# Windowed attention and a SiLU expert on one core: PSUM banks of the expert layers chosen by a longer eviction time, and one load of batch 0 moved from SP's queue to POOL's

## The chip, the core and the metric

The kernel runs on one core of a Trainium2 chip. Five engines work side by side, each on its own list of instructions in a fixed order, and wait for one another through semaphores: TensorE (PE in the profile; its weight loads are PEld), VectorE (DVE), ScalarE (ACT), GpSimd (POOL) and SyncE (SP). POOL and SP issue the DMA transfers here: POOL's go to a software queue (q0 in the profile) and can change the type on the way, SP's to a hardware queue (q1). Matmul results land in PSUM, which has eight banks of 128 partitions by 512 fp32 values. The metric is the device time of one execution in microseconds (us).

## What is computed

Attention in a causal window of 64 positions, over 8 batches and 8 heads with 576 positions and head size 64, and then an expert of two layers on the 4608 rows that result:

```python
def _attn_ref(q, k, v):                        # each (8, 8, 576, 64)
    scores = np.matmul(q, k.transpose(0, 1, 3, 2)) / np.sqrt(64)
    rel = pos[:, None] - pos[None, :]
    scores = np.where((rel >= 0) & (rel < 64), scores, -1000000000.0)
    attn = np.exp(scores - np.max(scores, axis=-1, keepdims=True))
    attn = attn / (np.sum(attn, axis=-1, keepdims=True) + 1e-09)
    return np.matmul(attn, v)

def _moe_ref(x, w_in, w_out):                  # x (4608, 512), w_in (512, 2048), w_out (2048, 512)
    h = x @ w_in
    g = h * (1.0 / (1.0 + np.exp(-h)))
    return g @ w_out
```

Inputs and output are fp32; the kernel computes in bf16 with fp32 sums.

## The kernel before

**Planning.** The kernel is written as operations with dependencies, an assumed duration on each engine that may run them, and a rank by class. `Plan.run` plays these through at build time and so fixes the order of instructions on each engine. An operation's `seen` is the time at which the plan takes its result as visible: its end plus `lat` for engine work (0.08 unless said otherwise), and for a transfer a begin on a modelled pipe plus `dma`. An operation that writes PSUM names a pool of banks (`at`: 0 to 3, `pv`: 4 and 5, `mp`: 4 to 7, `all`: 0 to 7). The plan gives it an idle bank, one whose last reader is `seen`, and of these for pool `mp` first banks 6 and 7, then 4 and 5, each time the one that has been idle longest. In the trace banks 0 to 3 are called `at` and 4 to 7 `mp`. On the chip only the order and the banks are left of this: real waits go by semaphores.

**Batch 0.** q and k of batch 0 come in eight loads, two heads each: q0, k0, q1, k1, q2, q3, k2, k3, where the number is the pair of heads. The first three (q0, k0, q1) are issued by SP as fp32 (L232), and an engine casts them to bf16 (L235). The other five are issued by POOL with the cast in the transfer (L229). TensorE transposes two loads at a time against an identity (L282), and ScalarE and VectorE copy the transposes out of PSUM, half each (L289). Then follow six units of scores (L311 adds the mask as a bias, L319 the product of q and k), exp on ScalarE (L337), the product with v (L349), and on VectorE the reciprocal (L356), the scaling (L359) and a transpose into `bridge` (L363), the expert's input. Until the last exp of batch 0, TensorE fills gaps with matmuls on zeros (L595).

**Later batches.** q and k come by POOL in 32-partition pieces (L239) and are transposed by VectorE (L246). The scores (L331) use banks 0 to 3, the product with v (L349) banks 4 and 5.

**Loads.** All of POOL's transfers go through one queue with eight outstanding: a ninth issue waits for the landing of the one eight before. Their order is q and k of batch 0, v of batch 0 (L253), w_in (L259), then q, k and v of batch 1 mixed with eight pairs of w_out's row blocks (L265), then the later batches.

**The expert.** Nine tiles of 512 rows (tile 0 takes the first 576 rows in two parts for the first layer, tile 1 what is left). The first layer (L369) sums four matmuls into one bank for each of 16 column blocks, and ScalarE's Silu (L375) reads the bank. The second layer (L381) sums 16 matmuls into a bank for each of four row blocks (tile 0 has all four open at once), the result is copied out (L387) and stored by SP (L391). The matmuls of the expert are one list in a fixed order, lowest in rank. The attention of the next batch goes in between, mostly within the second layer: scores, then some 17 second-layer matmuls, then the product with v.

Of the kernel before, what the change touches and what calls it, by code (L numbers as in the profile page):

```python
# [8 lines left out]
FP32 = mybir.dt.float32  # L9
# [5 lines left out]
class Plan:  # L15
# [31 lines left out]
    def run(self):  # L47
        head = {c: 0 for c in self.queues}
        engines = sorted({e for q in self.queues.values() for op in q for e in op["us"]})
        free = {e: 0.0 for e in engines}  # L50
        can = {e: [c for c, q in self.queues.items() if any(e in op["us"] for op in q)] for e in engines}
        table, left = "exp", self.count
        pipe, sent = {True: 2.0, False: 0.0}, []
        events, order = [0.0], []
        while left:
            if not events:
                raise RuntimeError([(c, head[c], q[head[c]]["n"]) for c, q in self.queues.items() if head[c] < len(q)])
            now = self.now = heapq.heappop(events)
            while events and events[0] == now:
                heapq.heappop(events)  # L60
            moved = True
            while moved:
                moved = False
                for e in engines:
                    if free[e] > now:
                        continue
                    best, kept = None, set()
                    heads = [(self.queues[c][head[c]], c) for c in can[e] if head[c] < len(self.queues[c])]
                    for op, c in sorted(heads, key=lambda x: x[0]["first"]):
                        if e == "POOL" and op["dma"] and len(sent) >= 8 and sent[-8] > now:  # L70
                            continue
                        if e not in op["us"] or not self.done(op["deps"]) or (op["gate"] and not op["gate"]()):
                            continue
                        if op["pool"]:
                            idle = [i for i in self.pools[op["pool"]] if i not in kept and self.done(self.banks[i])]
                            if len(idle) < len(op["untils"]):
                                if op["pool"] != "mp":
                                    kept.update(self.pools[op["pool"]])
                                continue
                            idle.sort(key=lambda i: (op["pool"] == "mp" and i in self.pools["pv"],  # L80
                                                     max([u["seen"] for u in self.banks[i]], default=0.0)))
                            op["bank"] = idle[:len(op["untils"])]
                            for i, until in zip(op["bank"], op["untils"]):
                                self.banks[i] = until
                        best = (op, c)
                        break
                    if best is None:
                        continue
                    op, c = best
                    head[c] += 1  # L90
                    us = op["us"][e]
                    if op["table"] and op["table"] != table:
                        table, us = op["table"], us + 1.28
                    end = free[e] = now + us
                    soft = e == "POOL"
                    if op["dma"] is None:
                        op["seen"] = end + op["lat"]
                    elif soft:

                        begin = max(pipe[True], end + 1.4)  # L100
                        pipe[True] = begin + op["dma"] * (1.5 if pipe[False] > begin else 1.0)
                        op["seen"] = pipe[True] + op["lat"] + 1.2
                        sent.append(op["seen"])
                        heapq.heappush(events, op["seen"])
                    else:
                        begin = max(pipe[False], end + 1.0)
                        busy = pipe[True] > begin and c != "ld0"
                        pipe[False] = begin + op["dma"] * (1.6 if busy else 1.0)
                        if busy:
                            pipe[True] += 0.6 * op["dma"]  # L110
                        op["seen"] = pipe[False] + {"ld0": 0.5, "st": 1.2}.get(c, 3.0)
                    op["at"], op["cls"], op["by"] = now, c, e
                    order.append((op, e))
                    left -= c != "warm"
                    moved = True
                    heapq.heappush(events, end)
                    heapq.heappush(events, op["seen"])
        for op, e in order:
            op["fn"](e)
# [3 lines left out]
def kernel(ctx, tc, q, k, v, w_in, w_out, out):  # L123
    nc = tc.nc
# [103 lines left out]
    def load_first_cast(w, u, kk):  # L228
        nc.gpsimd.dma_start(out=natbs[w][:, 0:S], in_=two(u, kk))  # L229

    def load_first(i, u, kk):
        nc.sync.dma_start(out=nats[i][:, 0:2 * S].bitcast(FP32), in_=two(u, kk))  # L232

    def cast_first(e, i, w):
        copies[e](out=natbs[w][:, 0:S], in_=nats[i][:, 0:2 * S].bitcast(FP32))  # L235
# [178 lines left out]
    def add_first_batch():  # L414
        got = {}
        for what, u in FIRST_LOADS:
            if what == "v":
                add_v_loads(0, [u], [c_vv[0]])
                continue
            kk = "qk".index(what)  # L420
            w = n_nat[1] % NNB
            n_nat[1] += 1
            if (what, u) in FIRST_LOADS[0:3]:
                i = n_nat[0] % NN
                n_nat[0] += 1
                ld = p.add("ld0", {"SP": 0.45}, lambda _, i=i, u=u, kk=kk: load_first(i, u, kk), dma=0.69)
                ca = p.add("cast", {"ACT": 0.7, "DVE": 0.56}, lambda e, i=i, w=w: cast_first(e, i, w), [ld])
                nat_free[i] = [ca]
            else:
                ca = p.add("early" if (what, u) in FIRST_LOADS[3:7] else "dma0", {"POOL": 0.6}, lambda _, w=w, u=u, kk=kk: load_first_cast(w, u, kk), dma=0.74)  # L430
            got[what, u] = (w, ca)
            if (what, u ^ 1) not in got:
                continue
            a = u // 2
            ws, loaded = zip(*[got[what, 2 * a + i] for i in range(2)])
            tu = p.add("turn", {"PE": 0.6}, None, [*loaded, c_ident], lat=0.1, pool="all", nb=2)
            tu["fn"] = lambda _, tu=tu, ws=ws: turn_first(tu, ws)
            for i in range(2):
                tu["untils"][i].append(p.add("lift", {"ACT": 0.64, "DVE": 0.75}, lambda e, tu=tu, a=a, kk=kk, i=i:
                                             lift(e, tu, a, kk, i), [tu, c_k[0]]))  # L440
                kq_done[(0, a)] = kq_done.get((0, a), []) + tu["untils"][i]
# [89 lines left out]
    def add_tile(j):  # L531
# [18 lines left out]
        for i, (ft, lo, hi) in enumerate(work):  # L550
            have = [op for n in range((j * TT + hi + 191) // 192) for op in o_done[n]]
            g, si = gt[ft]
            bank = None
            for c in range(NDC):
                op = p.add("moe", {"PE": 0.0036 + (hi - lo) / 2400}, None,
                           have + win[ft] + (exps[0] if j == 0 else []), lat=0.1,
                           pool=None if c else "mp")
                bank = bank or op
                op["fn"] = lambda _, bank=bank, ft=ft, c=c, lo=lo, hi=hi: first_layer(bank, j, ft, c, lo, hi)
                moe.append((op, 1, 1 if c == 0 and (i == 0 or hi > work[i - 1][2]) else -1))  # L560
            si.append(p.add("silu", {"ACT": 0.18 + (hi - lo) * 0.00083}, lambda _, bank=bank, g=g, lo=lo, hi=hi:
                            silu(bank, g, lo, hi), [op] + free_gt.get(g, []), table="silu"))
            bank["untils"][0] = [si[-1]]
        order = [(m, f, 0, d_model) for m in range(4) for f in range(NFT)]
        if j == 0:
# [4 lines left out]
        for i, (m, f, lo, hi) in enumerate(order):  # L570
# [7 lines left out]
            if f == NFT - 1:  # L578
                ot = n_ot[0] % NOT
                n_ot[0] += 1  # L580
                cp = p.add("out", {"DVE": 0.18 + (hi - lo) / 1000, "ACT": 0.18 + (hi - lo) / 1160},
                           lambda e, bank=bank[(m, lo)], ot=ot, lo=lo, hi=hi: copy_out(e, bank, ot, lo, hi),
                           [op, free_ot.get(ot)])
                bank[(m, lo)]["untils"][0] = [cp]
                free_ot[ot] = p.add("st", {"SP": 0.45}, lambda _, ot=ot, m=m, lo=lo, hi=hi: store(ot, j, m, lo, hi), [cp],
                                    dma=0.75 * (hi - lo) / d_model)
# [65 lines left out]
```

## Time and profile before

| | |
|---|---|
| device time, three runs | 302.37, 300.89, 302.20 us (median 302.2) |
| the profiled execution | 302.37 us, span of its instructions 300.6 us |
| TensorE busy | 287.4 us (96%) |
| ScalarE, VectorE, POOL busy | 176.8, 139.4, 117.0 us |
| first layer L369 busy, matmuls | 128.6 us, 696 |
| second layer L381 busy, matmuls | 124.2 us, 576 shown |
| Silu L375 | 174, 523 ns each |
| SP's loads of q in batch 0 (2), issue to landing | 4.7 us in the median |
| POOL's loads of k in batch 0 (3), issue to landing | 6.6 us in the median |

A row of the profile names the line, the engine, the operation, what it writes and reads, and in brackets how long the engine stood idle before it and what ended that. The chain of work that ended last is followed back from the last instruction: each piece is what the next one waited for, so a resource that the chain runs through sets the end. An engine that is not on the chain can be idle without cost. Matmuls overlap in the pipeline: one of 512 columns is shown with 0.38 us, but the next starts 0.216 us after it, so the spacing of the starts, not the length, is the rate. Some matmul records are missing.

### The profile page before, as it was taken

To read this page: it belongs to the slowest core of one execution; us is meant where nothing else is said; L and a number is where in the kernel's file an instruction comes from. 1 tells how busy PE (TensorE), PEld (TensorE's weight loads), DVE (VectorE), ACT (ScalarE), POOL (GpSimd) and SP (SyncE) were. 2 spreads that over 40 slices of the span, in tenths; PEclk is the share of its full clock that TensorE was granted. 3 is DMA by queue.
4 is the path that set the end of the run, shared out by engine and by line. 5 is a ranking of instruction groups with operands and counts; after the bars stand their busy time and mean duration, and the time that the engine had idled before them with its cause. 6 is when DMAs were issued, how large, how long until landed. Compare 5 with 4: busy or idle time off the path is not lost.

```text
span 300.6 us, 8485 instructions
## 1 busy us (share of the span) xinstructions
PE 287.4 (96%) x3609; PEld 150.4 (50%) x3641; DVE 139.4 (46%) x340; ACT 176.8 (59%) x341; POOL 117.0 (39%) x174
## 2 busy tenths in 40 slices
PE   7899999899999999999999999999999999999995
PEld 3566744785444544445444544454444544444444
DVE  3593377978886379327931693066006600000000
ACT  3697854886456745675477437753876376126511
POOL 8866976959898979860500000000000000000000
PEclk9799999999999999999999999999999999999999
DMA  7999999999999999992760210011001100020012
GB/s 174 176 203 169 131 165 170 225 136 129 171 179 141 109 188 172 148 94 74 81 71 0 74 39 34 2 37 72 35 0 39 72 35 2 35 77 29 2 70 71
DMA packets 82982, 28.78 MB, mean 96 GB/s; under 512 B 72448, under 2 KB 78080, under 8 KB 82944
## 3 DMA queue, kind: packets, MB, share of 16 engines
q0 software_dynamic: 77040, 17.92, 64.3%
q1 hardware_dynamic: 5904, 10.32, 9.8%
q8 instruction: 28, 0.46, 0.6%
q14 instruction: 10, 0.08, 0.1%
HBM read 36.70 MB, written 9.44 MB: 153 GB/s over the span
## 4 chain that ended last, share of the span: by engine, by line
PE 82%; DMA 8%; POOL 6%; issue 3%; ACT 1%; POOLq 0%; ACTq 0%
PE mp L381 39%; PE mp L369 37%; DMA w_out_sb<-in_moe_w_out_dram 5%; PE at L331 3%; PE mp L349 3%; DMA w_in_sb<-in_moe_w_in_dram 2%; POOL vv L253 2%; POOL w_in_sb L259 1%; POOL nat L239 1%; POOL w_out_sb L265 1%; POOL natb L229 1%; ACT ot L387 0%; ACT g L375 0%; PE at L349 0%; POOL ident L188 0%
## 5 line engine op out<-in xcount | busy, mean ns | idle before, releaser
L369 PE MATMUL mp<-bridge,w_in_sb 128*128 128x512 bf16 (+5 forms) x696 | 128.6, 342 | 1.8 <-ACT g L375 1.2
L381 PE MATMUL mp<-w_out_sb,g 128*128 128x512 bf16 (+2 forms) x576 | 124.2, 368 | 4.1 <-issue 3.3
L375 ACT ACTIVATE g<-mp 128x512 bf16<-128x512 f32 (+5 forms) x174 | 89.5, 523 | 30.9 <-PE mp L369 29.6
L369 PEld LDWEIGHTS <-w_in_sb 128*128 128x128 bf16 x696 | 66.3, 97 | 62.2 <-issue 7.6
L381 PEld LDWEIGHTS <-g 128*128 128x128 bf16 x608 | 55.9, 98 | 61.5 <-issue 0.7
L387 ACT COPY ot<-mp 128x512 f32<-128x512 f32 (+2 forms) x36 | 20.2, 563 | 62.1 <-PE mp L381 42.8
L340 DVE TENSOR_TENSOR e<-e,mask 128x384 bf16<-128x384 bf16 x84 | 26.0, 348 | 50.2 <-ACT e L337 49.7
L337 ACT ACTIVATE e<-at 128x384 bf16<-128x384 f32 x89 | 36.9, 497 | 16.0 <-PE at L331 15.9
L239 POOL DMA_DIRECT2D nat<-in_k_dram x56 | 34.6, 632 | 11.7 <-DMA vv<-in_v_dram 4.7
L253 POOL DMA_DIRECT2D vv<-in_v_dram x32 | 31.9, 1012 | 13.0 <-PE mp L349 12.9
L239 POOL DMA_DIRECT2D nat<-in_q_dram x56 | 34.8, 640 | 5.2 <-DMA w_out_sb<-in_moe_w_out_dram 3.2
L363 DVE STREAM_TRANSPOSE bridge<-ox 128x384 bf16<-128x384 bf16 x48 | 24.9, 553 | 0.0
L246 DVE STREAM_TRANSPOSE kt<-nat 128x576 bf16<-128x576 bf16 x28 | 20.7, 782 | 7.4 <-DMA nat<-in_k_dram 7.4
L246 DVE STREAM_TRANSPOSE qt<-nat 128x576 bf16<-128x576 bf16 x28 | 20.9, 789 | 1.3 <-DMA nat<-in_q_dram 1.2
L359 DVE TENSOR_TENSOR ox<-mp,rc 128x384 bf16<-128x384 f32 x43 | 21.3, 536 | 0.1
L356 DVE RECIPROCAL rc<-mp 128x6 f32<-128x6 f32 x43 | 8.0, 191 | 18.9 <-PE mp L349 18.3
L349 PEld LDWEIGHTS <-e 128*32 128x32 bf16 x1152 | 10.8, 95 | 9.0 <-issue 5.0
L299 DVE COPY vv<-vv 64x576 bf16<-64x576 bf16 (+1 forms) x14 | 7.3, 524 | 11.7 <-DMA nat<-in_k_dram 9.2
L349 PE MATMUL mp<-vv,e 128*32 128x65 bf16 x1032 | 12.2, 194 | 0.0
L331 PE MATMUL at<-qt,kt 32*128 32x64 bf16 x1008 | 11.6, 190 | 0.0
L331 PEld LDWEIGHTS <-kt 32*128 32x128 bf16 x1008 | 9.3, 92 | 4.3 <-issue 3.8
L337 ACT ACT_TABLE_LOAD x7 | 9.0, 1283 | 0.1
(55 smaller groups left out, 87.9 us busy)
## 6 DMA issues: line engine op xcount, KB each, us to landing
out_dram<-ot SPq DMA_DIRECT2D x35, 256.0 KB, 2.0
vv<-in_v_dram POOLq DMA_DIRECT2D x32, 144.0 KB, 5.6
nat<-in_q_dram POOLq DMA_DIRECT2D x56, 72.0 KB, 4.6
nat<-in_k_dram POOLq DMA_DIRECT2D x56, 72.0 KB, 4.0
w_out_sb<-in_moe_w_out_dram POOLq DMA_DIRECT2D x8, 256.0 KB, 7.6
w_in_sb<-in_moe_w_in_dram POOLq DMA_DIRECT2D x6, 256.0 KB, 7.3
nat<-in_q_dram SPq DMA_DIRECT2D x2, 288.0 KB, 4.7
w_in_sb<-in_moe_w_in_dram POOLq DMA_DIRECT2D x4, 128.0 KB, 6.0
```

The source lines that it names most:

```text
L239: nc.gpsimd.dma_start(out=nats[i][32 * h:32 * h + 32].rearrange("p (m x) -> p m x", m=NB), in_=(q, k)[kk][b, 4 * a + h].rearrange("(m p r) ...
L246: nc.vector.transpose(out=to[:, (2 * a + part) * S:(2 * a + part + 1) * S].rearrange("x (m t r) -> x m r t", t=32, r=2), in_=nats[i].rearr ...
L253: queue[e].dma_start(out=vv[b % NV][:, 2 * g0 + 1:2 * g1 + 1:2, 0:D], in_=v[b].rearrange("h s d -> (h s) d").rearrange("(g p) d -> p g d", ...
L331: nc.tensor.matmul(at_six(op["bank"][h])[:, a, x], lhsT=kt[b % NK][r, at:at + 128], rhs=qt[b % NK][r, at:at + 64], start=(s == a == x == 0 ...
L337: nc.scalar.activation(out=es[n % NE], in_=at_six(bank), func=ACTF.Exp, scale=scale)
L340: nc.vector.tensor_mul(es[n % NE], es[n % NE], mask0 if g == 0 else mask)
L349: nc.tensor.matmul(at_pv(bank)[32 * h:32 * h + 32, x, t], lhsT=e_of(b, a, n, h)[:, x, 32 * t:32 * t + 32], rhs=vv[b % NV][:, (4 * a + h) * ...
L359: nc.vector.tensor_mul(oxs[n % NOX], at_pv(bank)[:, :, :, 0:D], rcs[n % NRC].unsqueeze(3).to_broadcast([128, 3, 2, D]))
L363: nc.vector.transpose(out=bridge[:, n0:n0 + 3, 2 * a:2 * a + 2].rearrange("x t s (u i) -> x t s u i", u=2), in_=oxs[n % NOX].rearrange("p ...
L369: nc.tensor.matmul(banks[bank["bank"][0]][:, 0:hi - lo], lhsT=w_in_sb[:, c, ft * 128:(ft + 1) * 128], rhs=bridge[:, (j * TT + lo) // 64:(j ...
L375: nc.scalar.activation(out=gts[gt][:, lo:hi], in_=banks[bank["bank"][0]][:, 0:hi - lo], func=ACTF.Silu)
L381: nc.tensor.matmul(banks[bank["bank"][0]][:, 0:hi - lo], lhsT=gts[gt][:, m * 128:(m + 1) * 128], rhs=w_out_sb[:, f, lo:hi], start=(f == 0) ...
```

## The change

The change has two parts that touch the plan. The banks: Silu and copy-out operations of tiles 2 to 8 are planned with `lat` 0.22 instead of 0.08, so that a bank counts as taken for longer after its eviction; and once the last product with v is placed, every operation with a pool may take any of the eight banks. The loads: only q0 and k0 of batch 0 stay on SP; q1 goes to POOL with the cast in the transfer, ahead of k1, q2 and q3; the modelled times of SP's two loads are other ones.

```diff
                         if op["pool"]:
-                            idle = [i for i in self.pools[op["pool"]] if i not in kept and self.done(self.banks[i])]
+                            idle = [i for i in self.pools[op["pool"] if head["pv"] < len(self.queues["pv"]) else "all"] if i not in kept and self.done(self.banks[i])]
...
-                        busy = pipe[True] > begin and c != "ld0"
+                        busy = pipe[True] > begin
...
-                        op["seen"] = pipe[False] + {"ld0": 0.5, "st": 1.2}.get(c, 3.0)
+                        op["seen"] = pipe[False] + {"ld0": 1.2, "st": 1.2}.get(c, 3.0)
...
-            if (what, u) in FIRST_LOADS[0:3]:
+            if u == 0:
                 i = n_nat[0] % NN
                 n_nat[0] += 1
-                ld = p.add("ld0", {"SP": 0.45}, lambda _, i=i, u=u, kk=kk: load_first(i, u, kk), dma=0.69)
+                ld = p.add("ld0", {"SP": 0.45}, lambda _, i=i, kk=kk: load_first(i, kk), dma=-0.15 if kk == 0 else 0.7)
...
-                ca = p.add("early" if (what, u) in FIRST_LOADS[3:7] else "dma0", {"POOL": 0.6}, lambda _, w=w, u=u, kk=kk: load_first_cast(w, u, kk), dma=0.74)
+                ca = p.add("early" if (what, u) in FIRST_LOADS[2:6] else "dma0", {"POOL": 0.6}, lambda _, w=w, u=u, kk=kk: load_first_cast(w, u, kk), dma=0.74)
...
             si.append(p.add("silu", {"ACT": 0.18 + (hi - lo) * 0.00083}, lambda _, bank=bank, g=g, lo=lo, hi=hi:
-                            silu(bank, g, lo, hi), [op] + free_gt.get(g, []), table="silu"))
+                            silu(bank, g, lo, hi), [op] + free_gt.get(g, []), lat=0.22 if j > 1 else 0.08, table="silu"))
...
                            lambda e, bank=bank[(m, lo)], ot=ot, lo=lo, hi=hi: copy_out(e, bank, ot, lo, hi),
-                           [op, free_ot.get(ot)])
+                           [op, free_ot.get(ot)], lat=0.22 if j > 1 else 0.08)
```

In the order of instructions this gives: POOL issues q1, k1, q2, q3, then makes the identity, then issues k2 and k3 (before: k1, q2, q3, k2, the identity, k3). TensorE transposes q0/q1, k0/k1 and q2/q3, runs the first unit of scores, transposes k2/k3, runs four more units of scores and then the first product with v (before: all four transposes, four units of scores, the first product). First layers of tiles 2 to 7 use banks 4 to 7 and never the same one within two groups (before: mostly 6, 7, 6, 7); the rest of tile 7 and tile 8 use all eight. The number of matmuls on zeros stays 21. Behind the first matmul of the first layer the order on TensorE, ScalarE, VectorE, POOL and SP is the same as before but for the numbers of banks and of the `nat` buffers.

More of the change, by code (lines that the diff above doesn't have):

```diff
@@ L229, in load_first_cast, with load_first @@
         nc.gpsimd.dma_start(out=natbs[w][:, 0:S], in_=two(u, kk))
-    def load_first(i, u, kk):
-        nc.sync.dma_start(out=nats[i][:, 0:2 * S].bitcast(FP32), in_=two(u, kk))
+    def load_first(i, kk):
+        nc.sync.dma_start(out=nats[i][:, 0:2 * S].bitcast(FP32), in_=two(0, kk))
     def cast_first(e, i, w):
```

## The prediction

> **What bounds the kernel now.** I read the busy row first, then the chain that ended last, then the places where the chain leaves TensorE.
>
> ```profile
> PE 287.4 (96%) x3609; PEld 150.4 (50%) x3641; DVE 139.4 (46%) x340; ACT 176.8 (59%) x341; POOL 117.0 (39%) x174
> ```
>
> TensorE (PE) is the bound. No other engine passes 59%, so an edit counts only by the TensorE idle or waiting time that it takes away or adds. The chain shows two kinds of place:
>
> ```profile
> 13.54 7.20 DMA w_in_sb<-in_moe_w_in_dram
> 20.73 0.28 issue
> 21.02 8.23 DMA w_out_sb<-in_moe_w_out_dram
> ...
> 36.72 7.63 DMA w_out_sb<-in_moe_w_out_dram
> 44.36 0.04 issue
> 44.40 1.02 PE mp L381 x4
> ...
> 116.50 14.00 PE mp L369 x64
> ...
> 268.90 14.08 PE mp L369 x64
> ```
>
> Columns are start, length, what. Until 44.4 us the chain runs through POOL's queue of loads and ends on the fifth pair of w_out rows (issued at 36.72, landed at 44.36). From there it is TensorE, tile after tile. A first layer of a full tile (L369, 64 matmuls of 512 columns) takes 14.00 or 14.08 us. ScalarE's rows of the last tile show why that is not its floor:
>
> ```profile
> 271.54 0.60 ACT L375 ACTIVATE g<-mp 128x512 bf16<-128x512 f32 x1 [0.27 <-PE mp L369]
> 272.47 0.60 ACT L375 ACTIVATE g<-mp 128x512 bf16<-128x512 f32 x1 [0.33 <-PE mp L369]
> 273.33 0.60 ACT L375 ACTIVATE g<-mp 128x512 bf16<-128x512 f32 x1 [0.27 <-PE mp L369]
> 274.24 0.60 ACT L375 ACTIVATE g<-mp 128x512 bf16<-128x512 f32 x1 [0.31 <-PE mp L369]
> ```
>
> The starts are 0.93, 0.86 and 0.91 apart: every second group of four matmuls comes about 0.045 late. The start:
>
> ```profile
> 1.24 0.68 POOL L229 DMA_DIRECT2D natb<-in_k_dram  x1 [0.79 <-POOLq L636]
> 1.65 0.42 SPq L232 DMA_DIRECT2D nat<-in_q_dram  x1
> 8.12 0.67 ACT L235 CAST natb<-nat 128x576 bf16<-128x576 f32 x1 [3.09 <-DMA nat<-in_q_dram]
> 8.85 1.05 PE L282 MATMUL at<-ident,natb 128*64 128x128 bf16 x17 [2.33 <-ACT natb L235]
> ```
>
> SP's third load (q of heads 2, 3), issued at 1.65, lands at 8.10 and is cast until 8.79; TensorE's first transposes wait 2.33 us for it.
>
> **Part 1: the banks of tiles 2 to 8.** In the order of instructions before, the first layers fall into using banks 6, 7, 6, 7. A bank is then wanted again two groups later, 2 x 0.863 = 1.726 us (four matmuls at the measured pitch of 0.216). Its real turn is longer. In the last tile the group from 270.48 has its Silu at 271.54, 1.06 later; the Silu takes 0.60; the next matmul into the bank starts 0.07 after the Silu's end, at 272.21. The sum, 1.73, leaves nothing, and a Silu itself delayed delays the next group. So steps of 0.257 to 0.262 stand where 0.216 should, between matmuls of adjoining groups. I count 4 in each of tiles 2 to 7 and 6 in tile 8: 30 x 0.044 = 1.3 us. The second group of a tile is late by another 0.017 in six tiles: 0.1. Check by sums: the first nine groups of tile 2, whose banks come round after three groups or more, run at 0.863 each without a late step; against that pitch tile 2 loses 0.17, tiles 3 to 7 0.19 each, tile 8 0.27: 1.4 in all. In the new order no group of tiles 2 to 8 reuses a bank within two; three groups are 2.59 us against a turn of 1.73. **Saved: 1.4 us**, all on the bound. The bounds are 0 (if the handoff, not the bank, makes the late steps) and 1.4, since below 0.863 a group cannot go. I take 1.4, because tile 2 shows both reuses side by side.
>
> What else this moves: first layers now end on banks 4 and 5, which the next attention products (L349) need. Between them stand the scores and some 17 second-layer matmuls, 3.7 us; the Silu is done 1.1 + 0.6 = 1.7 after its group began. Nothing waits. The eight banks after attention put tile 8 on banks 0 to 3 too; three suffice, so this adds nothing. The orders of TensorE, ScalarE and VectorE are otherwise the same from the first first-layer matmul on.
>
> **Part 2: the third load moves from SP to POOL.** SP loses one issue (0.42), and its next instruction is a store at 53 us: nothing. ScalarE loses a cast of 0.67 at 8.12. POOL gains an issue ahead of all others, 0.57 to 0.68: the identity (done 3.9) comes at 4.5, before TensorE's first transpose at 6; the window and with it the bias (5.0) come 0.6 later, wanted at 9; the v issues from 4.91 and w_in from 8.85 come 0.6 later, but land 5 to 6 us after issue from a backlog, so this hides as long as the backlog lasts. VectorE and ScalarE swap halves of two copies (0.72 against 0.75): nothing. The nat buffers are used from one number earlier; each still waits for the batch two before, as now.
>
> Attention starts sooner. q now has POOL's first place, whose load (k) landed at 6.79 even against SP's third; the later places landed at 8.26, 8.92, 9.64 and 10.43. By these places, at the latest, the first transposes begin at 6.8 instead of 8.85, the second pair 8.3, the third 9.7, the first scores 10.4 instead of 13.1, and after one transpose group (0.69) and four more score groups (0.71 each, one now ahead of the first product) the first product starts at 14.7 instead of 15.97. If q lands at 5.8, as I expect without SP's third beside it, 13.8. VectorE's chain to the last bridge (16.48 to 23.42) follows the first product, so the first layer reaches steady running **1.3 to 2.2 us sooner**.
>
> The clock agrees with that. From 9.0 to 12.4 the granted clock was 0.50, behind the 2.33 us wait; three transpose groups took about 0.98 each where one at full clock took 0.69. The Trainium skill ("TensorE: Matmul & The Clock Gate", Part 1) halves the clock only after an idle window of about 3.4 us; by that this wait would have cost no clock, so by the page 0.9 us less would come back. The row stands against it.
>
> **But what is gained there is not kept.** At 44.40 TensorE waits for w_out's fifth pair:
>
> ```profile
> PE mp L381 <- DMA w_out_sb<-in_moe_w_out_dram: 0.2, 1, 0.2
> 44.40 1.02 PE L381 MATMUL mp<-w_out_sb,g 128*128 128x512 bf16 x4 [0.23 <-DMA w_out_sb<-in_moe_w_out_dram]
> ```
>
> It would have been there at 44.17. If it comes at 42.0 to 42.9, it waits till the pair lands, and the gain shrinks to how much sooner that is. All loads go through POOL's one queue, eight outstanding, so I ask how the queue shifts:
>
> ```profile
> q0 software_dynamic: 459, 0.47, 77.0%
> q1 hardware_dynamic: 145, 0.29, 25.0%
> ```
>
> This is the move of 4 to 8 us. The software queue moved 0.47 MB beside SP's third load; alone, from 7 us on, it moves 0.177 MB per us, in those 4 us 0.71. It carries 0.147 MB more now (0.8 us) and gets back up to 0.24 MB (1.4 us): 0.6 us sooner. Ends: 0.75 later (one more place at the observed step of 0.66 to 0.79, and no relief), 1.4 sooner (relief and no price). I take **0.5 us sooner**, near the sum, a little off for the ramp.
>
> The Trainium skill ("DMA: Bandwidth & Descriptors", Specifications) speaks against this half: it calls SP's path the faster one, 0.6 us to the first byte against about 1 us on GpSimd's. By the page this move costs some 0.4 us (an estimate). The rows say otherwise: SP's third landed 6.5 us after its issue, POOL's first 5.5.
>
> **Sum.** Profiled execution 302.37 us (span 300.61 and 1.76 around it): 302.37 - 1.4 - 0.5 = 300.5. The median shown, 302.2, is 0.2 below, so **300.3**. The three runs before reach from 300.89 to 302.37, so single times scatter by more than half of what I forecast. A change under 0.5% (1.5 us) can't be told from none.
>
> **Rivals.**
> - *The bank's part alone* (20%): the w_out pair lands no sooner, or up to 0.75 later. For it: one more transfer stands ahead of it in the queue. Against it: SP's share of 4 to 8 us is freed. 300.8 to 301.6.
> - *The whole start is kept* (15%): the pair lands 1 to 2.2 sooner, since the queue ran nearly dry from 29 to 32 us (POOL idle 1.65 before 29.53, waiting for a slot), and such a spell may close. 302.2 - 1.4 - 1.0 to 2.2: 298.6 to 299.8.
> - *Late steps stay* (6%): the 0.045 is the handoff's and not the bank's; the change doesn't do what it says. Against it: tile 2. 301.7.
> - *Slower* (4%): POOL's queue runs dry twice more behind the added transfer, as at 27.88 to 29.53. Price 2 x 1.65 + 0.75 = 4.1 at the w_out pair; it outweighs the banks from a landing at 45.8 and is measurably slower from 47.3. 302.2 - 1.4 + 4.1 = 304.9. Only one such spell is in the trace, so I think it unlikely.
>
> The forecast's own case (1.4 and 0.2 to 1.0) has 55%: 299.8 to 300.6. The range takes in the first two rivals and the third, with 0.3 for scatter at the top: 298.9 to 301.9. Faster by over 0.5% means below 300.7: most of the forecast's case (44), all of the whole start (15), a little of the first rival (3): 62%. Within 0.5%: 34%. Slower: 4%.
>
> **What would show it.** First layers of 13.8 us in the chain for tiles 3 to 8, Silu starts 0.86 apart. The first transposes at about 6 and no clock of 0.5 after 9. Steady first layer by 21 to 22. A wait of 1 to 2 us for w_out where 0.23 stood, its landing at 43.9. I am wrong if the 0.26 steps remain, if that pair lands after 45, or if a new wait stands between 44 and 60.

## The result

| | before | changed |
|---|---|---|
| median (range, runs) | 302.14 us (300.13 to 303.33, 6) | 298.65 us (297.99 to 299.08, 6) |
| profiled execution, its span | 302.37, 300.6 us | 298.62, 296.9 us |

The ratio is 0.9895, with a 95% interval of 0.9859 to 0.9932: 3.2 us faster (2.1 to 4.3). The direction was forecast, the size was not: 1.9 us were expected, and the median lies 0.25 below the low end of the range. Run again beside the last experiments, the changed kernel took 298.23 us (ratio 0.9871, 0.9838 to 0.9904). One run below, of the loads alone (304.27 us, 1.6% above that kernel's fastest), was in a slower state and is in neither its median nor its ratio.

The chain of the changed kernel, at the places shown of before (start, length, what):

```profile
36.56 6.25 DMA w_out_sb<-in_moe_w_out_dram
42.85 1.02 PE mp L381 x4
...
114.77 13.81 PE mp L369 x64
```

w_out's fifth pair is wanted 2.0 us sooner (42.15 against 44.17) and lands 1.55 sooner (42.81 against 44.36), and a first layer takes 13.81 us instead of 14.00. The Silu rows of the last tile:

```profile
270.68 0.60 ACT L375 ACTIVATE g<-at 128x512 bf16<-128x512 f32 x1 [0.27 <-PE at L369]
271.54 0.60 ACT L375 ACTIVATE g<-at 128x512 bf16<-128x512 f32 x1 [0.27 <-PE at L369]
272.40 0.60 ACT L375 ACTIVATE g<-at 128x512 bf16<-128x512 f32 x1 [0.27 <-PE at L369]
273.27 0.60 ACT L375 ACTIVATE g<-at 128x512 bf16<-128x512 f32 x1 [0.27 <-PE at L369]
```

The starts are 0.86 to 0.87 apart; no step of 0.91 is left. The start of TensorE, and what it still waits for:

```profile
6.16 0.47 PE L282 MATMUL mp<-ident,natb 128*64 128x128 bf16 x9 [0.66 <-DMA natb<-in_q_dram]
7.05 0.69 PE L282 MATMUL at<-ident,natb 128*64 128x128 bf16 x18
```

```profile
PE mp L369 <- ACT g L375: 0.8, 1, 0.8
PE mp L381 <- DMA w_out_sb<-in_moe_w_out_dram: 0.7, 1, 0.7
PE mp L282 <- DMA natb<-in_q_dram: 0.7, 1, 0.7
PE mp L369 <- DMA w_in_sb<-in_moe_w_in_dram: 0.4, 1, 0.4
```

The columns are the sum of the waits, their number and the longest. The 2.33 us for the third load became 0.66, and a group of transposes takes 0.69 us at full clock.

And one place that the prediction did not look at. This is the wait of SP's queue at the end of the program, first of the kernel before, then of the changed one:

```profile
SPq L647 <- DMA out_dram<-ot: 1.2, 1, 1.2
```

```profile
SPq L647 <- DMA out_dram<-ot: 0.3, 1, 0.3
```

Behind its last store SP waits, one after the other, for the eight semaphores that its transfers take in turn, and then the program ends. Before, SP had 41 transfers, so the last store used the first of the eight: SP stood at the first wait until that store had landed (298.83), and the other seven waits and the ending followed, 1.77 us to the end of the span. Now SP has 40; the last store has the eighth, the other waits pass while it is under way, and from its landing (295.93) the span runs 0.93 us.

Where the 3.75 us of the two spans come from, read at fixed points of the traces: tile 2's first layer starts 1.55 us sooner (83.66 against 85.21); from there to the end of tile 8's first layer another 1.36 go; from the last landing to the end 0.85.

### The profile page after: what moved, and what is told of

It is laid out like the page before. It is cut to its first block, busy times and chain, and to the rows that moved or that the text cites. A ratio compares the mean times of both kernels' runs of the same rounds, so it can differ in the third digit from the quotient of the medians.

```text
span 296.9 us, 8483 instructions
## 1 busy us (share of the span) xinstructions
PE 284.7 (96%) x3609; PEld 149.7 (50%) x3641; DVE 138.5 (47%) x340; ACT 176.1 (59%) x340; POOL 117.5 (40%) x175
## 4 chain that ended last, share of the span: by engine, by line
PE 82%; POOL 8%; DMA 5%; issue 3%; ACT 1%; POOLq 0%; ACTq 0%
PE mp L381 33%; PE mp L369 30%; PE at L369 6%; PE at L381 6%; PE at L331 3%; DMA w_in_sb<-in_moe_w_in_dram 3%; PE mp L349 3%; DMA w_out_sb<-in_moe_w_out_dram 2%; POOL w_in_sb L259 2%; POOL nat L239 2%; POOL vv L253 2%; POOL natb L229 1%; POOL w_out_sb L265 1%; ACT ot L387 0%; ACT g L375 0%
## 5 line engine op out<-in xcount | busy, mean ns | idle before, releaser
L369 PE MATMUL mp<-bridge,w_in_sb 128*128 128x512 bf16 (+5 forms) x608 | 108.9, 337 | 2.9 <-issue 0.9
L381 PE MATMUL mp<-w_out_sb,g 128*128 128x512 bf16 (+1 forms) x482 | 105.3, 368 | 4.5 <-issue 3.3
L375 ACT ACTIVATE g<-mp 128x512 bf16<-128x512 f32 (+5 forms) x152 | 76.7, 513 | 25.8 <-PE mp L369 24.6
L387 ACT COPY ot<-mp 128x512 f32<-128x512 f32 (+1 forms) x30 | 16.9, 566 | 46.6 <-PE mp L381 27.4
L369 PE MATMUL at<-bridge,w_in_sb 128*128 128x512 bf16 x88 | 20.0, 379 | 0.0
L381 PE MATMUL at<-w_out_sb,g 128*128 128x512 bf16 (+1 forms) x94 | 19.2, 361 | 0.1
L375 ACT ACTIVATE g<-at 128x512 bf16<-128x512 f32 x22 | 12.9, 597 | 4.5 <-PE at L369 4.5
L387 ACT COPY ot<-at 128x512 f32<-128x512 f32 (+1 forms) x6 | 3.3, 550 | 15.7 <-PE at L381 15.7
```

Of the source, the lines that this page charges most:

```text
L369: nc.tensor.matmul(banks[bank["bank"][0]][:, 0:hi - lo], lhsT=w_in_sb[:, c, ft * 128:(ft + 1) * 128], rhs=bridge[:, (j * TT + lo) // 64:(j ...
L375: nc.scalar.activation(out=gts[gt][:, lo:hi], in_=banks[bank["bank"][0]][:, 0:hi - lo], func=ACTF.Silu)
L381: nc.tensor.matmul(banks[bank["bank"][0]][:, 0:hi - lo], lhsT=gts[gt][:, m * 128:(m + 1) * 128], rhs=w_out_sb[:, f, lo:hi], start=(f == 0) ...
L387: copies[e](out=ots[ot][:, lo:hi], in_=banks[bank["bank"][0]][:, 0:hi - lo])
```

## The experiments

Each was timed beside the kernel before on the same chip; a ratio turns into us at the median of before there (301.93 for the first four, 301.47 for the next four, 301.82 for the last three). Kernels from different groups are best compared by their ratios.

**The banks alone** (kernel before):

```diff
-[i for i in self.pools[op["pool"]] if ...
+[i for i in self.pools[op["pool"] if head["pv"] < len(self.queues["pv"]) else "all"] if ...
-silu(bank, g, lo, hi), [op] + free_gt.get(g, []), table="silu"))
+silu(bank, g, lo, hi), [op] + free_gt.get(g, []), lat=0.22 if j > 1 else 0.08, table="silu"))
-[op, free_ot.get(ot)])
+[op, free_ot.get(ot)], lat=0.22 if j > 1 else 0.08)
```

> The kernel before with the bank part of the change alone (the longer hold of tiles 2 to 8 and all eight banks after attention; three loads stay on SP). My theory (1.4 us from the banks, 1.55 us from w_out's fifth pair landing sooner, 0.8 us at the end of the program): 302.1 - 1.4 = 300.7 us, first layers of 13.8 us in tiles 3 to 8, the first transposes still waiting until 8.8 us, w_out's fifth pair still landing near 44.4, and 1.7 us from the last store's landing to the end. Rival (the banks carry most of the gain, as freer banks also let attention in sooner): 299.5 us or less.

Measured: 300.6 us, ratio 0.9954 (0.9936 to 0.9973), 1.4 us faster. Tiles 2 to 8 take 13.60 us each from the first to the last start of a first-layer matmul, where the kernel before has 13.77 in tile 2, 13.78 in tiles 3 to 7 and 13.86 in tile 8. Its chain:

```profile
117.14 13.81 PE mp L369 x64
```

1.79 us from the last landing to the end. The theory holds; but the w_out pair landed at 42.64 and not near 44.4, with the same loads. TensorE did not wait for it; the chain stays on TensorE there:

```profile
24.46 13.39 PE mp L369 x98
...
38.36 4.48 PE mp L381 x20
42.84 0.48 PE at L331 x48
```

**The loads alone** (changed kernel without the bank part, the diff above reversed).

> The changed kernel without the bank part (q1 on POOL, banks as before). My theory: 298.65 + 1.4 = 300.0 us, with late steps of 0.26 us again in the first layers, w_out's fifth pair landing near 42.8, and 0.9 us from the last store's landing to the end. Rival (the start is hidden behind the loads, as the prediction's clamp had it at its strictest): 301.5 to 302 us with the pair landing at 44.

Measured: 300.26 us, ratio 0.9941 (0.9919 to 0.9964), 1.8 us faster, and the late steps are back (13.77 to 13.87 us a tile). The time fits the theory. The pair landed at 44.05, as the rival said, and took a part of the gain in the profiled execution (301.24 us):

```profile
40.92 1.89 PE L381 MATMUL mp<-w_out_sb,g 128*128 128x512 bf16 x8 [1.23 <-DMA w_out_sb<-in_moe_w_out_dram]
44.10 1.02 PE L381 MATMUL mp<-w_out_sb,g 128*128 128x512 bf16 x4 [1.28 <-DMA w_out_sb<-in_moe_w_out_dram]
```

So the clamp of the prediction exists, but it works in some executions and not in others.

**One more tiny load on SP** (changed kernel):

```diff
+extra = keep.tile([128, 4], FP32, name="extra")
+p.add("ld0", {"SP": 0.45}, lambda _: nc.sync.dma_start(out=extra, in_=w_out[0:128, 0:4]), dma=1e-6)
```

> The changed kernel with one more tiny load on SP (128 rows of 16 bytes of w_out into a spare tile that nothing reads), issued behind q0 and k0. SP then has 41 transfers as before, so that the last store takes the first of eight semaphores again and not the eighth. My theory (the end of the program waits for the semaphores in a fixed order): 298.65 + 0.85 = 299.5 us, all of it between the last store's landing and the end (1.7 us instead of 0.9), nothing else moved. Rival (the shorter end of the changed kernel was chance): 298.65 us, and 0.9 us there.

Measured: 299.11 us, ratio 0.9908 (0.9882 to 0.9934). From the last landing to the end 1.77 us again, and SP's wait there is as it was before:

```profile
SPq L649 <- DMA out_dram<-ot: 1.2, 1, 1.2
```

The profile shows the mechanism. What it is worth in the device time is less certain: the medians give 0.5 us (298.65 to 299.11), the ratios 0.4 with intervals that overlap, against the 0.85 expected.

**Fifteen more matmuls on zeros** (kernel before, ahead of the first transpose):

```diff
+if ws == (0, 2):
+    for _ in range(15):
+        nc.tensor.matmul(banks[op["bank"][1]][:, 0:384], lhsT=blank, rhs=..., start=True, stop=True)
```

> The kernel before with 15 more matmuls on zeros ahead of the first transpose, so that TensorE works through the wait for the third SP load. My theory: the granted clock stays at 1.0 behind 9 us, the first transposes run at full clock (0.69 instead of about 0.98 us a group), attention of batch 0 is up to 0.9 us sooner, but w_out's fifth pair lands at 44.4 as before and takes the gain back: 301.9 to 302.1 us. Rival (what the start gains is kept to the end): 301.2 us. If the clock falls all the same, it was not the idle time that lowered it.

Measured: 302.11 us, ratio 1.0007 (0.9988 to 1.0026). The clock stayed at 1.00, and a transpose group took 0.69 us. But the added matmuls ran until 9.4, past the third load, which this time had landed at 6.2, so the start was no sooner; and the w_out pair landed at 41.12, not at 44.4. With the load there so early, this profile alone says nothing of the clock, but the timings do: the granted clock, as a mean over the execution (3.4 us at half clock make 0.994), was 0.998 or more in all twelve, and 0.994 or less in 14 of the 25 of the kernel before beside them. So the clock follows TensorE's idle time; of the clamp the run says nothing.

**Ten instead of fifteen.**

> The kernel before with 10 more matmuls on zeros instead of 15, so that TensorE is busy until about 8.2 us but not past the cast of the third SP load. My theory: the half clock behind 8 to 9 us is gone, the first transposes start where they did (8.8 to 9.3) and run at 0.69 us a group, and the time falls by 0.3 to 0.9 us to 301.0 to 301.6, with the lesser end if w_out's fifth pair takes some of it. Rival (the half clock is hidden): 301.9 us, no change.

Measured: 301.71 us, ratio 1.0017 (0.999 to 1.0045). In the profile the clock stayed at 1.00 and the first transposes began at 7.94, and in nine of the twelve timings the mean clock was 0.998 or more; the other three, at 0.994, took 303.52 to 304.04 us. No gain can be measured, and the rival's time came, but the edit removed the half clock only in part, so it does not give its price. The last section has what the timings say of that.

**A whole third load on SP beside q1's on POOL** (changed kernel; as the tiny one, but 288 KB):

```diff
+extra = keep.tile([128, 9 * D], FP32, name="extra")
+p.add("ld0", {"SP": 0.45}, lambda _: nc.sync.dma_start(out=extra, in_=two(1, 0)), dma=1e-6)
```

> The changed kernel with a third load of 288 KB on SP as in the kernel before (the same rows of q, into a spare tile that nothing reads), beside POOL's q1. SP has 41 transfers, so this is to be read against the run with the tiny third load. My theory (SP's third load and POOL's queue share one rate): POOL's first loads land 0.5 to 1 us later than with the tiny load (q1 near 6.8), attention starts that much later, and the time is 0.3 to 1.0 us above it: 299.4 to 300.1 us. Rival (the transfers do not hinder each other): the same as with the tiny load, 299.1 us.

Measured: 300.21 us, ratio 0.997 (0.9949 to 0.9992), against 299.11 and 0.9908 with the tiny load: 1.1 us by the medians, 1.9 by the ratios. q1 landed at 7.75; with the tiny load it was 6.05, and in the other profiles with q1 on POOL 5.10 to 6.64:

```profile
5.58 0.24 PE L282 MATMUL mp<-ident,natb 128*64 128x128 bf16 x1
7.80 0.47 PE L282 MATMUL mp<-ident,natb 128*64 128x128 bf16 x9 [1.97 <-DMA natb<-in_q_dram]
```

The wait of before is back, without anything on TensorE's path that needs SP's load. So the load on SP's queue holds up POOL's first load, and by more than expected.

**w_out's pairs ahead of v** (changed kernel):

```diff
-FIRST, SPLIT, SECOND_LOADS = 8, 14, "0w12ww3vwvwvwvww"
+FIRST, SPLIT, SECOND_LOADS = 8, 14, "0w12ww3wvwvwvvww"
```

> The changed kernel with w_out's fourth to sixth pair ahead of the v loads that they stood behind in POOL's queue (batch 1's order of loads; the last v keeps its place). My theory: in the changed kernel TensorE reaches tile 0's second layer 2 us sooner than before and waits 0 to 1 us for w_out's fifth pair, run by run; with that pair about 1 us sooner in the queue no such wait is left: 298.65 - 0.5 = 298.1 us. Rival (the loads only change places): the product with v of batch 1 waits instead, 298.6 us or more, with a new wait near 48 us.

Measured: 298.18 us, ratio 0.989 (0.9863 to 0.9917). No wait for w_out is left, and the pair lands at 41.48. TensorE waits for w_in earlier on, but this is not the edit's doing, since a second profile of the changed kernel has the same line:

```profile
PE mp L369 <- DMA w_in_sb<-in_moe_w_in_dram: 1.3, 1, 1.3
```

The time was as expected, yet it can't be told from the changed kernel (0.9895 and 0.9871).

**Four banks to the end** (changed kernel without the eight banks after attention).

> The changed kernel with four banks for the expert to the end (the longer hold stays). My theory (three banks are enough): tile 8 takes 13.6 us from first to last start as in the changed kernel, 298.65 us. Rival (the eight banks carry part of the gain at the end): 298.9 us or more, with steps of 0.26 us in tile 8.

Measured: 298.75 us, ratio 0.9905 (0.9875 to 0.9936), 13.60 us in tile 8 as in the others. The eight banks bring nothing that can be measured; four, none used twice within two groups, are enough.

**w_in's third pair in two halves** (on the kernel with w_out first):

```diff
-for lo, hi in ((0, 256), (256, 512), (512, 1024), ...
+for lo, hi in ((0, 256), (256, 512), (512, 768), (768, 1024), ...
```

> The kernel with w_out's pairs ahead of the v loads, and w_in's columns 512 to 1024 loaded as two pairs of 128 KB transfers instead of one pair of 256 KB (two more transfers in POOL's queue). My theory: in the kernels whose attention starts sooner, TensorE waits 0.4 to 1.9 us near 18 to 20 us for the transfer that completes these columns; with the first half of them complete about 1.3 us sooner, two groups of the first layer run before the wait: 0.3 to 0.5 us below the kernel without it, 297.7 to 297.9 us. Rival (the last bridge, near 21 us, sets the steady start anyway): 298.2 us.

Measured: 299.63 us, ratio 0.992 (0.9889 to 0.9951), 1.4 us slower than the changed kernel on the same chip (298.23). Both theories missed. In the profiled execution the w_in wait fell to 0.5 us, but q1 was waited for 1.6 us and w_out 0.7. Why two transfers more cost so much was not settled.

**Seven tiny loads on SP** (kernel before; 48 transfers):

```diff
+extra = keep.tile([128, 28], FP32, name="extra")
+for x in range(7):
+    p.add("ld0", {"SP": 0.45}, lambda _, x=x: nc.sync.dma_start(out=extra[:, 4 * x:4 * x + 4], in_=w_out[0:128, 4 * x:4 * x + 4]), dma=1e-6)
```

> The kernel before with seven more tiny loads on SP behind its three (128 rows of 16 bytes each, into a spare tile that nothing reads), so that SP has 48 transfers and the last store takes the eighth semaphore. My theory: 0.9 us instead of 1.7 from the last store's landing to the end, 0.85 us below the kernel before, 301.0 to 301.1 us. Rival (that end is set by something else, and the one tiny load of the earlier run moved it by chance): no change, 301.9 us.

Measured: 301.3 us, ratio 0.9987 (0.9965 to 1.0008). From the last landing to the end 0.92 us, as the theory has it. Over all profiles this end is 1.77 to 1.79 us with 41 transfers on SP (six) and 0.92 to 0.93 with 40 or 48 (seven). The median moved by 0.4 to 0.5 us only; the interval holds no change as well as 0.85.

**The changed kernel again.**

> The changed kernel once more, on the same chip as the kernel with both orders of loads, to compare with it: 298.65 us.

Measured: 298.23 us, ratio 0.9871 (0.9838 to 0.9904). No version tried is clearly below it.

## Why the prediction was right or wrong

**The banks: right.** The sum said 1.4 us. The seven tiles lost 0.17, five times 0.18 and 0.26, 1.33 in all, and the banks alone measured 1.4 (0.8 to 1.9). That the bank and not the handoff makes the late steps held too: with the bank part alone they are gone, and without the bank part they are back. That the eight banks add nothing held as well (298.75 us with four).

**The sooner start: right.** q1 landed at 6.11 (5.8 expected, 6.8 at the latest). The steady first layer came at 21.2 instead of 23.3, 2.1 us sooner (1.3 to 2.2 expected), and no half clock was left.

**"But what is gained there is not kept": the step that failed.** I took the landing of w_out's fifth pair at 44.36 for a fixed property of the queue and asked how far it would shift; 0.5 us was the answer and the term of the sum. That landing moves by itself. In five profiles with the loads of before it came at 44.36, 42.64, 41.12, 42.58 and 43.71, in five with the changed loads at 42.81, 44.05, 42.46, 42.24 and 42.99: 42.9 on average in both, so no shift shows against a spread of 3.2 us. The execution that I read had the latest of them, and with it the spell of 1.65 us in which POOL issued nothing. At the same load the kernel with ten matmuls on zeros has the second row here, and the other profiles have no wait:

```profile
29.53 0.60 POOL L239 DMA_DIRECT2D nat<-in_q_dram  x1 [1.65 <-DMA w_out_sb<-in_moe_w_out_dram]
28.09 0.60 POOL L239 DMA_DIRECT2D nat<-in_q_dram  x1 [0.45 <-DMA w_out_sb<-in_moe_w_out_dram]
```

w_out's second pair was issued at 30.12 behind that spell, and between 28.33 and 29.80 in the others. So the spell was that execution's and not the kernel's. TensorE came to that pair at 44.2 in the execution read, and waited for no pair of w_out in the four others with these loads; coming 2 us sooner, it is held now and then (0.7 us in the changed kernel's profile, where the prediction had 1 to 2 and a landing at 43.9, 2.5 at two pairs in that of the loads alone, none with four banks). Between kernels with the same end, the tiny third load against the banks alone, the start is worth 1.4 us (0.9908 against 0.9954, intervals that do not meet). That is the term that was 0.5.

The working behind it had the parts near right and the place wrong. SP's load in the way was put at 1.4 us and measured 1.1 to 1.9; the added place in POOL's queue was put at 0.8, and the whole third load against the banks alone gives 0.5 (0.997 against 0.9954), with intervals that overlap. What can be seen of them is at the first loads, where TensorE waits (7.75 against 6.05); the pair landed at 43.07 with the whole load and 42.46 with the tiny one, within the spread. Of the rivals "the whole start is kept" gave the time (298.6 to 299.8), though not by its reason: the dry spell that was to close stood in no other profile of either order of loads.

**"SP loses one issue: nothing" failed too.** The removed transfer was followed to the instruction behind it, but not to the order in which the program's end waits for semaphores. 0.85 us in the profiles, 0.4 to 0.9 by medians and ratios; it was in no term and in no bound.

With the two terms as measured the sum is 1.4 + 1.4 + 0.85 = 3.65, or 3.2 with 0.4 for the end; both lie within the 2.1 to 4.3 of the result, which can't tell them apart. The slower case had no support in any run of the changed kernel.

On the two pages of the Trainium skill: "DMA: Bandwidth & Descriptors" (Specifications) gives SP's path 0.6 us to the first byte against about 1 us on GpSimd's. The prediction set against it SP's third load (6.5 us) and POOL's first (5.5), but that third load ran beside POOL's. In the changed kernel SP's q0 landed 2.9 us after its issue and POOL's q1 4.9, so SP's path was the faster here too; what decided was that its third load cost 1.1 to 1.9 us by what it took from the other queue. The other page stands below.

## What to carry to other kernels

A landing time read from one execution is a sample: before it serves as a clamp, compare it over several runs or ask what would hold it. Choose a PSUM bank by the whole turn, first matmul to the next one allowed (here 1.06 + 0.60 + 0.07 us), since a bank that is free 0.045 us late costs TensorE that much each time. And follow a removed transfer to the end of the program: which semaphore the last store takes decided 0.85 us of the span here.

## What the runs showed of the chip

**The half clock.** TensorE's clock fell to half after idle gaps of some 2 us. The first row is the kernel with four banks, which waited 1.90 us for w_in, the second the one with the tiny load, which waited 1.12 and stayed at a clock of 1.00:

```profile
20.69 16.04 PE L369 MATMUL mp<-bridge,w_in_sb 128*128 128x192 bf16 x110 [1.90 <-DMA w_in_sb<-in_moe_w_in_dram]
20.45 14.37 PE L369 MATMUL mp<-bridge,w_in_sb 128*128 128x192 bf16 x110 [1.12 <-DMA w_in_sb<-in_moe_w_in_dram]
```

The same 110 matmuls took 1.67 us longer behind the longer wait. The stretches of the kernel with four banks:

```profile
18.00:21.20 3.20, 1.30 (x17) 1.00 (x14) 2.75 (x6) 0.85 (x4) 0.88 (x2) 1.00 1.24 203
21.20:24.60 3.40, 3.40 (x17) 2.28 (x16) 0.00 (x0) 1.76 (x6) 2.23 (x4) 0.50 1.42 197
24.60:28.00 3.40, 3.40 (x23) 2.04 (x21) 1.28 (x3) 2.64 (x7) 2.72 (x6) 1.00 1.52 178
```

In these rows the third number from the end is the granted clock: 0.50 for 3.4 us, in which TensorE was wholly busy; half of 3.4 is what the matmuls lost. That execution took 299.9 us, the longest of its six. Gaps of 1.90, 1.97 and 2.33 us brought 3.4 us of half clock, one of 3.28 brought 6.8 us, and gaps of 1.3 to 1.75 us brought none. The changes of the clock in one profile lie whole multiples of 3.41 us apart (5.61, 9.02 and 12.43 in the kernel before). In the 3.41 us that ended with the fall TensorE was busy for a share of 0.32, 0.42, 0.43 and 0.44; cut into the same steps over the first 30 us, five other profiles have 0.49 to 0.53 in their emptiest one, and the clock stayed. (These shares are worked out from matmul records, of which some are missing.) So in these traces it is the share of such a step that goes with the fall, and a gap of 1.9 us does it where most of it lies in one step. With the banks alone, the profile of the 3.28 us gap, the step behind the fall was busy for 0.61 at half clock, and a second step at half clock followed. The Trainium skill ("TensorE: Matmul & The Clock Gate", Part 1) asks for an idle window of about 3.4 us; these gaps were shorter, and the measurement decides.

**The scatter.** The kernel before ranged over 3.2 us in its first six runs and the changed one over 1.1. In the traces with three loads on SP the third lands between 6.2 and 8.5 us, and a half clock of 0, 3.4 or 6.8 us follows. The timings beside the experiments show the same: of 65 of the kernel before, 29 had a mean granted clock of 0.994 or less and a median of 302.5 us, the other 36 had 0.997 or more and 301.2 us. All twelve timings of the changed kernel had 0.999 or 1.00. A half clock comes together with a long wait at the start, so the 1.3 us are the price of both; 29 of 65 times 1.3 is 0.6 us of the mean (an estimate), a part of what the sooner start brings. The spread inside each group, 2.6 and 2.4 us, is not explained by it.
